# First batch's row products: all four sums kept in their own accumulators, with negated tables, instead of half sums that are joined afterwards

## The chip, the cores and the metric

The kernel runs on one core of a Trainium2 chip. The metric is the time of one execution on the device, in microseconds (us). The kernel before takes 310.63 us, the median of three runs (310.2 to 311.31). The profile is one such execution; its span, from the first to the last instruction, is 308.7 us.

## The reference, cut to what matters

Attention in chunks of 32 positions, then a Fourier mix, then a two-layer network, for 4 batches of 768 positions and 512 channels (8 heads of 64).

```python
for c in range(S // 32):                       # attention: chunk 32, 16 left, 8 right, 8 memory rows
    k_full = concat([mem_k, k[..., l_start:r_end, :]])
    v_full = concat([mem_v, v[..., l_start:r_end, :]])
    a = softmax(q_c @ k_full.T / sqrt(D))
    out[c_start:c_end] = a @ v_full
x = out.transpose(0, 2, 1, 3).reshape(B, S, 512)
mixed = real(fft(fft(x, axis=1), axis=2))      # Fourier mix over positions and channels
u = x + mixed
un = (u - mean(u)) / sqrt(var(u) + 1e-6)
y = u + max(un @ w_ch1, 0) @ w_ch2             # 512 -> 2048 -> 512
```

## The kernel before

A planner lists tasks with an engine, an estimated cost, what they come after and which buffers they take and give. It places them with a simple clock of its own and so fixes the order of each engine's program; nothing else of its clock reaches the chip. Six accumulator banks are shared by turns, value products, row and column products and the network. A pair is two heads; pairs 0 to 3 are the first batch, 4 to 7 the second, and so on. `...` marks cuts.

```python
# loads: q and k on GpSimd's DMA queue, v on SyncE's
lq = add("POOL", 0.8, lambda: e_load_q(n), [behind1, kept.get("lk"), ...], take=("qf",), moved=1.5, rank=10 * n)
lk = add("POOL", 0.8, lambda: e_load_k(n), [lq], take=("kf",), moved=1.5, rank=10 * n + 1)
lv = [add("SP", ..., lambda hh=hh: e_load_v(n, hh), ..., moved=1.6 if n < HP else 0.9) for hh in range(2)]
# GpSimd copies 32 rows of v so that neighbouring chunks overlap
ov = [add("POOL", 0.84, lambda hh=hh: e_overlap(n, hh), [lv[hh], calm], margin=mgl) for hh in range(2)]
tq = add("PE", 0.40, lambda: e_turn_q(n), [lq, ...], give=("qf",), ...)    # turns of q and k
tk = add("PE", 0.43, lambda: e_turn_k(n), [lk, ..., tq], give=("kf",), ...)
...                                                                        # scores, exp
v_ = add("PE", 0.85, lambda g=g: e_values(n, g), x_ + ov, take=("xa",), ...)   # value products
t_norm[n, g] = add("DVE", 0.78, lambda g=g: e_norm(n, g), [v_, ...])

def load_w1(after):   # four quarters on GpSimd's queue, after the last overlap copy of pair 3
    return [add("POOL", 0.7, ..., [after], moved=2.2, rank=-1) for dt in range(NDT)]
def load_w2(after):   # four quarters, into the buffer that pair 3's v held
    return [add("POOL", 0.7, lambda g=g: e_w2(g), [after], moved=2.2, rank=-1) for g in range(4)]
```

The Fourier mix is a matrix product over positions (row products, with cosine and sine tables) and one over channels (column products). Symmetry folds the channels, which gives an even (`par` 0) and an odd (`par` 1) part, and a cosine (`ab` 0) and a sine (`ab` 1) part of each. The folded values are split into a high and a low 16-bit half (`hi`, `lo`), and so are the row sums (`up` and its remainder). In the first batch the channels come in two halves `h`: pairs 0 and 3 first, pairs 1 and 2 after. The second half's sums enter the even and odd parts with equal or opposite signs.

```python
def row_products(out_, parts, ab, tab, c0, c1, first=True, last=True):
    for sp in range(2):
        for st in range(3):
            for i, part in enumerate(parts):           # hi, lo: 12 matmuls of 193 columns
                nc.tensor.matmul(out_[:, sp, :], part[:, ab, sp * 3 + st, c0:c1], tab[:, sp, st, :], ...)

def e0_edge():                                         # one row each, at channels 128 and 384
    for par, tab in ((0, cosS), (1, sinS)):
        row_products(ps_of["own", par, 1][0:1], [e128...], par, tab, 0, 1)

def e0_rows(key, ab, h):
    ps_of[key] = ps = bank([P, 2, NK], FP32, "ps0")
    row_products(ps, hl_of[0, h], ab, cosS if ab == 0 else sinS, 0, P)

def e0_keep(key, ab):                                  # first half's sums to an SBUF buffer
    nc.scalar.copy(t_of[0][:, ab, key[1]], ps_of.pop(key))
def e0_join(par, ab):                                  # plus or minus the second half's sums
    op = ALU.add if par == ab else ALU.subtract
    nc.vector.tensor_tensor(t_of[0][:, ab, par], t_of[0][:, ab, ab and par], ps_of["other", ab], op)
def e0_up(par, ab): ...                                # ScalarE: high half of the joined sums
def e0_rest(par, ab): ...                              # VectorE: remainder
```

After the column products come the residual sums with the mean (VectorE), `un` (ScalarE), four turns of `un` per tile of 128 positions (TensorE), their copies `unT`, and the network: `ph` (first products, 64 matmuls of 384 columns per half batch), relu (ScalarE), `pc` (second products, 16 of 512 columns per tile), `osb`, and the store. The network's products have the lowest rank on TensorE and fill it wherever nothing else can run. Before the network has started, dummy `warm` matmuls fill planned gaps.

Of the kernel before, what the change touches and what calls it, by code (L numbers as in the profile page):

```python
# [10 lines left out]
FP32 = mybir.dt.float32  # L11
# [24 lines left out]
class Plan:  # L36
# [13 lines left out]
    def add(self, engine, cost, emit, after=(), take=(), give=(), rank=None, moved=0.0,  # L50
            fill=False, margin=0.0):
        t = dict(engine=engine, cost=cost, emit=emit, after=[a for a in after if a is not None],
                 take=take, give=give, rank=len(self.tasks) if rank is None else rank,
                 moved=moved, fill=fill, margin=margin, last_fill=False, done=None, at=None, no=len(self.tasks),
                 bank=None)
        self.tasks.append(t)
        return t
# [77 lines left out]
def kernel(  # L135
# [15 lines left out]
    P = 128  # L151
# [41 lines left out]
    def bank(shape, dtype, name):  # L193

        return bps.tile(shape, dtype, tag="bank%d" % plan.current["bank"], name=name)
# [34 lines left out]
    cosD = wpool.tile([P, 2, HD], FP16)  # L230
    nsinD = wpool.tile([P, 2, HD], FP16)
    sinD = wpool.tile([P, 2, HD], FP16)
    c384 = cpool.tile([P, NST], FP32)
    e128 = cpool.tile([P, 2, 2, NST], FP16)
    w1_sb = wpool.tile([P, NDT, DFF], FP16)
# [271 lines left out]
# [3 lines that stand above are left out]
                for i, part in enumerate(parts):  # L510
                    nc.tensor.matmul(out_[:, sp, :], part[:, ab, sp * 3 + st, c0:c1],  # L511
                                     tab[:, sp, st, :], start=(first and sp + st + i == 0),
                                     stop=(last and sp + st + i == 4))
# [55 lines left out]
    def e0_edge():  # L569

        for par, tab in ((0, cosS), (1, sinS)):
            row_products(ps_of["own", par, 1][0:1],
                         [e128[:, i].unsqueeze(3) for i in range(2)], par, tab, 0, 1)

    def e0_ff_edge(h):

# [14 lines left out]
            nc.vector.tensor_tensor(ff[:, ab, :, 1:P], rev_ap(pq, P - 1, P - 1, [[HD, NST]]),  # L591
                                    pq[:, :, P + 1:HD], op)

    def e0_rows(key, ab, h):

        ps_of[key] = ps = bank([P, 2, NK], FP32, "ps0")
        row_products(ps, hl_of[0, h], ab, cosS if ab == 0 else sinS, 0, P)

    t_of = []

    def e0_keep(key, ab):
        if not t_of:
            t_of.append(fpool.tile([P, 2, 2, 2, NK], FP32, tag="unT", bufs=2, name="join"))
        nc.scalar.copy(t_of[0][:, ab, key[1]], ps_of.pop(key))

    def e0_join(par, ab):
        op = ALU.add if par == ab else ALU.subtract
        nc.vector.tensor_tensor(t_of[0][:, ab, par], t_of[0][:, ab, ab and par],
                                ps_of["other", ab], op)

    def e0_up(par, ab):
        up = fpool.tile([P, 2, NK, 2], FP16, tag="up", bufs=4, name="up")
        up_of[0, par, ab] = [up.rearrange("p i k s -> p i (k s)"), None, up]
        nc.scalar.copy(up[:, 0].rearrange("p k s -> p s k"), t_of[0][:, ab, par])

    def e0_rest(par, ab):
        up = up_of[0, par, ab][2]
        nc.vector.tensor_tensor(up[:, 1].rearrange("p k s -> p s k"), t_of[0][:, ab, par],
                                up[:, 0].rearrange("p k s -> p s k"), ALU.subtract)

    def e0_columns(kt, ab):

# [169 lines left out]
    def e_table_rows():  # L792

        for tab, par, s0 in ((nsinD, 0, 1.0), (sinD, 0, 1.0), (nsinD, 1, -1.0), (sinD, 1, 1.0)):
            nc.gpsimd.memset(tab[0:1, par, 0:HD:2], s0)
            nc.gpsimd.memset(tab[0:1, par, 1:HD:2], -s0)

    t_sines = []
    for i, nm in enumerate("SSD"):
        t_sines.append(add("ACT", (1.35, 1.35, 1.8)[i], lambda i=i: e_sines(i), [t_angle[nm]]))  # L800
# [4 lines left out]
    for i in range(1, NV + 1):  # L805
        t_ones[i] = add("DVE", 0.1, lambda i=i: e_ones(i),
                        [t_col, t_clear["va", i, 0], t_clear["va", i, 1]])
    t_idh = add("DVE", 0.25, lambda: nc.vector.tensor_copy(ident_h, ident), [t_id], rank=142)


# [6 lines left out]
    def attention(n):  # L817
# [6 lines left out]
        kept["lk"] = lk  # L824
        lv = [add("SP", 2.1 if hh == 0 else 1.4, lambda hh=hh: e_load_v(n, hh),
                  [t_clear.get(("va", n, 0)), t_clear.get(("va", n, 1))], rank=10 * n + 2 + hh,
                  take=("va",) if hh == 0 and n != HP - 1 else (), moved=1.6 if n < HP else 0.9) for hh in range(2)]
        first = b == 0
        calm = kept["f0"] if b == 1 else None
        mgp, mg, mgl = SPARE[b]  # L830
# [8 lines left out]
                 margin=mgp)  # L839
        kept["tk"] = tk  # L840
        mk = add("DVE", 0.2, lambda: e_mkT(n),
                 [t_mkT, kept.get("mk"), t_clear["kTb", n] if n < NKT else None,
                  kept["f0"] if n == HP + 1 else None], take=("kTb",),
                 rank=len(plan.tasks) + 400 if b == 1 else None)
        kept["mk"] = mk
        ek = add("ACT", 0.85, lambda: e_kT(n), [tk, mk], give=(("tr", tk),), margin=mg)
# [49 lines left out]

    def load_w1(after):
        return [add("POOL", 0.7, lambda dt=dt: nc.gpsimd.dma_start(
            w1_sb[:, dt, :], moe_w_ch1[ts(dt, P), :]), [after], moved=2.2, rank=-1)
            for dt in range(NDT)]  # L900

    def e_w2(g):
        if g == 0:
            w2_of.append(wpool.tile([P, NHT, DM], FP16, tag="w2", name="w2_sb"))
        nc.gpsimd.dma_start(w2_of[0][:, ts(g, 4), :], w2v[:, ts(g, 4), :])  # L905

    def load_w2(after):
        return [add("POOL", 0.7, lambda g=g: e_w2(g), [after], moved=2.2, rank=-1)
                for g in range(4)]


# [28 lines left out]
    def part_of_first(add, t_rest):  # L940
        nrm = [[t_norm[i, g] for g in range(2)] for i in range(HP)]
        ff = hi = None
        rows, keep, t_join = {}, {}, {}
        for h in range(2):
            pq = [None]
            for i in range(2):
                pq.append(add("DVE", 1.15, lambda h=h, i=i: e0_pq(h, i),
                              nrm[2 * h + i] + [pq[-1]], take=("fold",) if i == 0 else ()))
            prev = pq[-1]
            if h == 1:  # L950
                ed = add("POOL", 0.8, e0_edge_parts, [pq[1]], rank=-3)
                ed = add("PE", 1.94, e0_edge, [ed, rows["own", 0, 1], rows["own", 1, 1]])
                for par in range(2):
                    own = rows["own", par, 1]
                    keep[par, 1] = add("ACT", 0.6, lambda par=par: e0_keep(("own", par, 1), 1),
                                       [ed], give=(("acc", own),))
            fe = add("DVE" if h else "POOL", 0.25 if h else 0.4, lambda h=h: e0_ff_edge(h),
                     [pq[-1]], take=("fold",), rank=None if h else -4)
            for ab in range(2):
                ff = add("DVE", 0.95, lambda h=h, ab=ab: e0_ff(h, ab), [fe, prev],  # L960
                         give=("fold",) if ab == 1 else ())
                prev = ff
                ht = ("hT", "hl")[h]
                hi = add("ACT", 0.85, lambda h=h, ab=ab: e_hi(0, h, ab), [ff, hi],
                         take=(ht,) if ab == 0 else ())
                lo = add("DVE", 0.96, lambda h=h, ab=ab: e_lo(0, h, ab), [hi],
                         give=("fold",) if ab == 1 else ())
                more = [kept["tk0"]] + t_sines if h == 0 else []
                for par in range(2 if (h, ab) == (0, 1) else 1):
                    key = ("own", par, ab) if h == 0 else ("other", ab)  # L970
                    end = (h, ab) == (1, 1) or (h, ab, par) == (0, 1, 1)
                    rows[key] = add("PE", 1.1, lambda h=h, ab=ab, key=key: e0_rows(key, ab, h),
                                    [lo] + more, take=("acc",), give=(ht,) if end else ())
            if h == 0:
                keep[0, 0] = add("ACT", 0.6, lambda: e0_keep(("own", 0, 0), 0), [rows["own", 0, 0]],
                                 take=("unT",), give=(("acc", rows["own", 0, 0]),))
                t_norm[2, 1]["after"].append(ff)
        join = up = None
        for ab in range(2):
            other = rows["other", ab]  # L980
            for par in (1 - ab, ab):
                t_join[par, ab] = join = add(
                    "DVE", 0.6, lambda par=par, ab=ab: e0_join(par, ab),
                    [keep[ab and par, ab], other, join],
                    give=(("acc", other),) if par == ab else ())
        for ab in range(2):
            for par in (1 - ab, ab):
                up = add("ACT", 0.5, lambda par=par, ab=ab: e0_up(par, ab), [t_join[par, ab], up],
                         take=("up",))
                t_rest[par, ab] = add("DVE", 0.45, lambda par=par, ab=ab: e0_rest(par, ab), [up],  # L990
                                      give=("unT",) if par and ab else ())
        kept["f0"] = lo

    def fourier(b):
# [149 lines left out]
```

## Time and profile before

| what | value |
|---|---|
| time, median of 3 runs | 310.63 us |
| span of the profiled run | 308.7 us |
| TensorE busy | 290.8 us (94%) |
| VectorE, ScalarE, GpSimd busy | 176.8, 167.8, 69.7 us |
| warm matmuls | 182, 14.4 us |
| ps matmuls (row products) | 264 |
| DMA moved | 24.49 MB, mean 79 GB/s |

The busy time of TensorE is a sum of instructions; the slices show where it is spent. The mean of 79 GB/s hides that nearly all loads come in the first quarter of the span. The chain of waits that ended last gives 76% of the span to TensorE and 8% to DMA, nearly all of that to `w_sb`, the weights' loads; and the chain is listed in order of time, so one can see where that share lies. An idle time in a row is the time of that engine just before the row's instructions, with what ended it; the releaser is inferred.

### The profile page before, as it was taken

Reading aid. Unit: us, or ns where it says so; the run is one execution under the profiler, and the core shown is the slowest. Engines: PE = TensorE matmul, PEld = TensorE weight load, DVE = VectorE, ACT = ScalarE, POOL = GpSimd, SP = SyncE. Lnnn points to the kernel's source line nnn. Section 1 sums busy time; section 2 is a strip of 40 time slices with the busy share of each in tenths; the row PEclk is TensorE's granted clock in tenths of the full one; section 3 lists DMA queues with packets and bytes.
Section 4 is the critical chain, followed back from the end, with each engine's and each line's share of the span. In section 5 each row is a group of like instructions: output and inputs, shape, how many; then the busy total and the mean of one; then the engine's idle time right before and its main releaser. Section 6 shows DMA issues by size and latency. Waiting matters only on the chain.

```text
span 308.7 us, 7849 instructions
## 1 busy us (share of the span) xinstructions
PE 290.8 (94%) x3327; PEld 193.9 (63%) x3327; DVE 176.8 (57%) x364; ACT 167.8 (54%) x300; POOL 69.7 (23%) x121
## 2 busy tenths in 40 slices
PE   8697999199999999999999999999999999999995
PEld 8586887076565756866668755767564554554644
DVE  7949978433149993689988989837800101002002
ACT  9966585437756388484585634652371360540720
POOL 7567721454352730032400020000100000000000
PEclk9999999669999999999999999999999999999999
DMA  6999999987679420033300001000100101101001
GB/s 84 166 159 202 195 200 196 199 151 119 94 149 192 98 55 2 2 95 83 101 2 2 2 34 71 0 2 34 46 24 34 71 0 55 49 0 68 36 34 68
DMA packets 42313, 24.49 MB, mean 79 GB/s; under 512 B 30375, under 2 KB 38823, under 8 KB 42279
## 3 DMA queue, kind: packets, MB, share of 16 engines
q0 software_dynamic: 9344, 10.49, 21.5%
q1 hardware_dynamic: 29479, 7.34, 13.0%
q10 hardware_dynamic: 3456, 6.16, 5.3%
q8 instruction: 26, 0.43, 0.6%
q14 instruction: 8, 0.07, 0.1%
HBM read 28.11 MB, written 6.29 MB: 111 GB/s over the span
## 4 chain that ended last, share of the span: by engine, by line
PE 76%; DMA 8%; DVE 7%; ACT 3%; issue 2%; POOL 2%; POOLq 0%
PE ph L685 27%; PE pc L699 24%; PE xa L437 7%; DMA w_sb<-in_moe_w_ch_dram 7%; PE pm L546 5%; PE ps L511 5%; PE sc L382 2%; PE tp L664 1%; ACT e L425 1%; PE trq L346 1%; PE trk L361 1%; DMA qf<-in_q_dram 1%; PE pc_half L707 1%; DVE lo L504 1%; POOL w_sb L905 1%
## 5 line engine op out<-in xcount | busy, mean ns | idle before, releaser
L692 ACT ACTIVATE hT<-ph 128x384 f16<-128x384 f32 x128 | 62.1, 491 | 66.0 <-PE ph L685 64.1
L685 PE MATMUL ph<-unT,w_sb 128*128 128x384 f16 x512 | 89.4, 328 | 0.7 <-ACT hT L692 0.6
L699 PE MATMUL pc<-w_sb,hT 128*128 128x512 f16 x368 | 84.8, 379 | 0.6 <-DVE unT L670 0.6
L685 PEld LDWEIGHTS <-w_sb 128*128 128x128 f16 x512 | 48.4, 98 | 33.4 <-issue 2.0
L699 PEld LDWEIGHTS <-hT 128*128 128x128 f16 x368 | 34.5, 98 | 38.3 <-issue 0.6
L727 DVE SCALAR_TENSOR_TENSOR osb<-pc,rstd,xsb 128x512 f32<-128x512 f32 x23 | 17.2, 748 | 71.7 <-PE pc L699 71.6
L339 POOL COPY va<-va 32x780 f32<-32x780 f32 x30 | 29.6, 1007 | 35.6 <-DMA va<-in_v_dram 35.1
L437 PE MATMUL xa<-va,e 128*64 128x65 f32 x720 | 28.0, 231 | 7.5 <-POOL va L339 6.6
L437 PEld LDWEIGHTS xa<-va,e 128*64 128x64 f32 x720 | 24.4, 143 | 12.7 <-POOL va L339 7.4
L390 ACT ACTIVATE e<-sc,mbias 128x384 f32<-128x384 f32 x48 | 25.2, 577 | 10.3 <-PE sc L382 9.8
L658 ACT ACTIVATE un<-xsb,mu_s 128x512 f16<-128x512 f32 x18 | 12.8, 720 | 15.7 <-DVE mu_s L652 15.6
L447 DVE RECIPROCAL zs<-xa 128x6 f32<-128x6 f32 x32 | 6.1, 189 | 21.7 <-PE xa L437 21.6
L448 DVE TENSOR_TENSOR xsb<-xa,zs 128x384 f32<-128x384 f32 x32 | 17.8, 558 | 1.1
L676 POOL TENSOR_SCALAR rstd<-mu_s 128x6 f32<-128x6 f32 x4 | 1.0, 245 | 70.7 <-DVE osb L727 42.0
L651 DVE BATCH_NORM_STATS2 st<-xsb 128x6 f32<-128x512 f32 x24 | 16.6, 690 | 0.6
L499 ACT CAST hi<-ff 128x768 f16<-128x768 f32 x14 | 11.4, 830 | 9.3 <-DVE ff L488 7.8
L310 POOL DMA_DIRECT2D qf<-in_q_dram x16 | 10.6, 660 | 23.7 <-PE trq L346 14.5
L504 DVE TENSOR_TENSOR lo<-ff,hi 128x768 f16<-128x768 f32 x14 | 14.4, 1042 | 2.4 <-ACT hi L499 2.4
L460 PE MATMUL warm<-zeros 128*128 128x128 bf16 x182 | 14.4, 242 | 1.0 <-DVE zero L247 1.0
L645 DVE TENSOR_TENSOR xsb<-pm,xsb 128x512 f32<-128x512 f32 x18 | 12.1, 672 | 5.2 <-PE pm L546 5.2
L351 ACT COPY qT<-trq 128x768 bf16<-128x768 bf16 x14 | 11.1, 795 | 6.4 <-PE sc L382 5.7
L371 ACT COPY kTb<-trk 128x832 bf16<-128x832 bf16 x16 | 13.4, 854 | 0.4 <-DVE osb L727 0.4
(147 smaller groups left out, 398.5 us busy)
## 6 DMA issues: line engine op xcount, KB each, us to landing
out_dram<-osb ACTq DMA_DIRECT2D x23, 256.0 KB
va<-in_v_dram SPq DMA_DIRECT2D x30, 176.0 KB
w_sb<-in_moe_w_ch_dram POOLq DMA_DIRECT2D x8, 512.0 KB, 13.2
qf<-in_q_dram POOLq DMA_DIRECT2D x16, 192.0 KB, 4.3
kf_all<-in_k_dram POOLq DMA_DIRECT2D x16, 192.0 KB, 5.8
va<-in_mem_v_dram SPq DMA_DIRECT2D x30, 24.0 KB
va<-in_v_dram SPq DMA_DIRECT2D x15, 28.0 KB
last<-in_v_dram SPq DMA_DIRECT2D x2, 176.0 KB
```

Source lines behind the costliest of these rows:

```text
L339: nc.gpsimd.tensor_copy(v1[0:32, 1:NB, 0:D + 1], v1[96:128, 0:NT, 0:D + 1])
L390: nc.scalar.activation(e1[:, :, :, ts(half, 32)], sc[:, :, 0:6, ts(half, 32)], AFT.Exp, bias=mbias[:, half:half + 1], scale=1.0 / math.sqr ...
L437: nc.tensor.matmul(xa[64 * half:64 * half + 64, st, hh, 0:65], e1[:, hh, t6, :], v1[:, 6 * g + t6 + 1, 0:65], start=True, stop=True)
L448: nc.vector.tensor_tensor(xs[b][:, 3 * g:3 * g + 3, 2 * pr * D:(2 * pr + 2) * D] .rearrange("p s (h d) -> p s h d", h=2), xa[:, :, :, 0:D] ...
L504: nc.vector.tensor_tensor(lo[:, ab].rearrange(fl), ff_of[b, par][:, ab].rearrange(fl), hi[:, ab].rearrange(fl), ALU.subtract)
L511: nc.tensor.matmul(out_[:, sp, :], part[:, ab, sp * 3 + st, c0:c1], tab[:, sp, st, :], start=(first and sp + st + i == 0), stop=(last and ...
L546: nc.tensor.matmul(pm[:, par, :], lhs, rhs[:, par, :], start=(im == 0), stop=(im == 3))
L651: nc.vector.bn_stats(st6, xs[b][:, kt, :])
L685: nc.tensor.matmul(ph[:, 0:384], w1_sb[:, dt, ts(ht, P)], unT_of[b][:, dt, sh * 384:(sh + 1) * 384], start=(dt == 0), stop=(dt == NDT - 1))
L692: nc.scalar.activation(hT_of[b, sh][:, ht, :], ph_of.pop((b, sh, ht))[:, 0:384], AFT.Relu, bias=0.0, scale=-1.0)
L699: nc.tensor.matmul(pc_of[b, sh, stl], hT_of[b, sh][:, ht, ts(stl, P)], w2_of[0][:, ht, :], start=(ht == 0), stop=(ht == NHT - 1))
L727: nc.vector.scalar_tensor_tensor(osb, pc_of.pop((b, sh, stl)), rstd_of[b][:, st:st + 1], xs[b][:, st, :], ALU.mult, ALU.add)
```

## The change

Each half of the first batch now makes all four row products (`par`, `ab`) of its own, and the second half adds to the first half's accumulators. Where the second half must enter with the opposite sign, its products take a negated table, made once at the start. So the copies to SBUF and the joins go, and the split reads the accumulators directly, as in the later batches. The two edge rows are added between the halves into the same accumulators. The planner's figures for the weights' and v's transfer times are other ones, and the memory keys' copy of pair 5 no longer waits for the first batch's last split.

```diff
     def e0_edge():
         for par, tab in ((0, cosS), (1, sinS)):
-            row_products(ps_of["own", par, 1][0:1],
-                         [e128[:, i].unsqueeze(3) for i in range(2)], par, tab, 0, 1)
+            row_products(ps_of[0, par, 1][0:1],
+                         [e128[:, i].unsqueeze(3) for i in range(2)], par, tab, 0, 1,
+                         False, False)
...
-    def e0_rows(key, ab, h):
-        ps_of[key] = ps = bank([P, 2, NK], FP32, "ps0")
-        row_products(ps, hl_of[0, h], ab, cosS if ab == 0 else sinS, 0, P)
-    def e0_keep(key, ab): ...
-    def e0_join(par, ab): ...
-    def e0_up(par, ab): ...
-    def e0_rest(par, ab): ...
+    def e0_rows(par, ab, h):
+        if h == 0:
+            ps_of[0, par, ab] = bank([P, 2, NK], FP32, "ps0")
+        ps = ps_of[0, par, ab]
+        turned = h == 1 and par != ab
+        tab = neg_of[0][:, ab] if turned else (cosS if ab == 0 else sinS)
+        row_products(ps, hl_of[0, h], ab, tab, 0, P, h == 0, h == 1)
...
+    def e_neg(i):
+        if i == 0:
+            neg_of.append(fpool.tile([P, 2, 2, 3, NK], FP16, tag="unT", bufs=2, name="neg"))
+        nc.vector.tensor_scalar(neg_of[0][:, i]..., (cosS, sinS)[i]..., -1.0, None, ALU.mult)
...
+    t_neg = [add("DVE", 0.4, lambda i=i: e_neg(i), t_sines[:2], rank=140 + i,
+                 take=("unT",) if i == 0 else ()) for i in range(2)]
...
         lv = ...
-                  ..., moved=1.6 if n < HP else 0.9) for hh in range(2)]
+                  ..., moved=1.6) for hh in range(2)]
...
         mk = add("DVE", 0.2, lambda: e_mkT(n),
-                 [t_mkT, kept.get("mk"), t_clear["kTb", n] if n < NKT else None,
-                  kept["f0"] if n == HP + 1 else None], take=("kTb",),
+                 [t_mkT, kept.get("mk"), t_clear["kTb", n] if n < NKT else None], take=("kTb",),
...
-            w1_sb[:, dt, :], moe_w_ch1[ts(dt, P), :]), [after], moved=2.2, rank=-1)
+            w1_sb[:, dt, :], moe_w_ch1[ts(dt, P), :]), [after], moved=3.2, rank=-1)
...
-        return [add("POOL", 0.7, lambda g=g: e_w2(g), [after], moved=2.2, rank=-1)
+        return [add("POOL", 0.7, lambda g=g: e_w2(g), [after], moved=3.5, rank=-1)
...
-                for par in range(2 if (h, ab) == (0, 1) else 1):
-                    key = ("own", par, ab) if h == 0 else ("other", ab)
-                    rows[key] = add("PE", 1.1, ..., [lo] + more, take=("acc",), ...)
-            if h == 0:
-                keep[0, 0] = add("ACT", 0.6, ...)
-                t_norm[2, 1]["after"].append(ff)
-        ...                          # joins, then splits, then remainders
+                for par in range(2):
+                    rows[par, ab] = rw = add(
+                        "PE", 1.0, lambda h=h, par=par, ab=ab: e0_rows(par, ab, h),
+                        [lo] + ([kept["v0" if (par, ab) == (1, 1) else "tk0"]] + t_sines if h == 0 else
+                                [rows[par, ab], t_neg[ab], ed]),
+                        take=("acc",) if h == 0 else (), ...)
+                    if h == 0:
+                        held[par, ab] = rw
+                    else:
+                        up = add("ACT", 0.6, lambda ...: e_up(0, par, ab), [rw], take=("up",))
+                        t_rest[par, ab] = add("DVE", 0.6, lambda ...: e_rest(0, par, ab), [up],
+                                              give=(("acc", held[par, ab]),))
```

More of the change, by code (lines that the diff above doesn't have):

```diff
@@ L232 @@
     sinD = wpool.tile([P, 2, HD], FP16)
+    neg_of = []
     c384 = cpool.tile([P, NST], FP32)
@@ L592, in e0_ff @@
                                     pq[:, :, P + 1:HD], op)
-    def e0_rows(key, ab, h):
-        ps_of[key] = ps = bank([P, 2, NK], FP32, "ps0")
-        row_products(ps, hl_of[0, h], ab, cosS if ab == 0 else sinS, 0, P)
[L599 to L619, printed above, removed]
+    def e0_rows(par, ab, h):
[5 more added lines that the diff above has]
+        row_products(ps, hl_of[0, h], ab, tab, 0, P, h == 0, h == 1)
     def e0_columns(kt, ab):
@@ L796, in e_table_rows @@
             nc.gpsimd.memset(tab[0:1, par, 1:HD:2], -s0)
+    def e_neg(i):
+        if i == 0:
+            neg_of.append(fpool.tile([P, 2, 2, 3, NK], FP16, tag="unT", bufs=2, name="neg"))
+        fl = "p a b c -> p (a b c)"
+        nc.vector.tensor_scalar(neg_of[0][:, i].rearrange(fl), (cosS, sinS)[i].rearrange(fl),
+                                -1.0, None, ALU.mult)
     t_sines = []
@@ L826, in attention @@
                   [t_clear.get(("va", n, 0)), t_clear.get(("va", n, 1))], rank=10 * n + 2 + hh,
-                  take=("va",) if hh == 0 and n != HP - 1 else (), moved=1.6 if n < HP else 0.9) for hh in range(2)]
+                  take=("va",) if hh == 0 and n != HP - 1 else (), moved=1.6) for hh in range(2)]
         first = b == 0
@@ L942, in part_of_first @@
         ff = hi = None
-        rows, keep, t_join = {}, {}, {}
+        rows = {}
+        held = {}
         for h in range(2):
@@ L951, in part_of_first @@
                 ed = add("POOL", 0.8, e0_edge_parts, [pq[1]], rank=-3)
[L952 to L956, printed above, removed]
+                ed = add("PE", 1.94, e0_edge, [ed, rows[0, 1], rows[1, 1]])
             fe = add("DVE" if h else "POOL", 0.25 if h else 0.4, lambda h=h: e0_ff_edge(h),
@@ L967, in part_of_first @@
                          give=("fold",) if ab == 1 else ())
-                more = [kept["tk0"]] + t_sines if h == 0 else []
-                for par in range(2 if (h, ab) == (0, 1) else 1):
-                    key = ("own", par, ab) if h == 0 else ("other", ab)
-                    end = (h, ab) == (1, 1) or (h, ab, par) == (0, 1, 1)
-                    rows[key] = add("PE", 1.1, lambda h=h, ab=ab, key=key: e0_rows(key, ab, h),
-                                    [lo] + more, take=("acc",), give=(ht,) if end else ())
@@ L974, in part_of_first @@
-            if h == 0:
-                keep[0, 0] = add("ACT", 0.6, lambda: e0_keep(("own", 0, 0), 0), [rows["own", 0, 0]],
-                                 take=("unT",), give=(("acc", rows["own", 0, 0]),))
-                t_norm[2, 1]["after"].append(ff)
[L978 to L991, printed above, removed]
+                for par in range(2):
+                    rows[par, ab] = rw = add(
+                        "PE", 1.0,
+                        lambda h=h, par=par, ab=ab: e0_rows(par, ab, h),
+                        [lo] + ([kept["v0" if (par, ab) == (1, 1) else "tk0"]] + t_sines if h == 0 else
+                                [rows[par, ab], t_neg[ab], ed]),
+                        take=("acc",) if h == 0 else (),
+                        give=((ht,) if par == 1 and ab == 1 else ()) +
+                        (("unT",) if (h, par, ab) == (1, 1, 1) else ()))
+                    if h == 0:
+                        held[par, ab] = rw
+                    else:
+                        up = add("ACT", 0.6, lambda par=par, ab=ab: e_up(0, par, ab), [rw],
+                                 take=("up",))
+                        t_rest[par, ab] = add("DVE", 0.6, lambda par=par, ab=ab:
+                                              e_rest(0, par, ab), [up], give=(("acc", held[par, ab]),))
```

## The prediction

> **What bounds the kernel now.** I read the page's forty slices first, then windows cut at the places where the slices change, then the chain of waits, then the timelines of TensorE and GpSimd around the one hole. From the page:
>
> ```profile
> PE   8697999199999999999999999999999999999995
> PEclk9999999669999999999999999999999999999999
> DMA  6999999987679420033300001000100101101001
> ```
>
> TensorE is full from slice 9 to the end. Before that it has one hole, slice 7 (about 54 to 62 us), and the granted clock drops there and in the slice after. The DMA engines are full from slice 1 to slice 7. Windows with the columns stretch, length, busy times of PE, PEld, DVE, ACT, POOL, granted clock, DMA share, GB/s:
>
> ```profile
> 54.36:60.68 6.32, 0.00 (x0) 0.00 (x1) 3.12 (x10) 2.95 (x6) 2.14 (x4) 0.69 1.22 198
> 60.68:66.70 6.02, 5.72 (x72) 4.54 (x72) 2.96 (x8) 1.16 (x3) 3.91 (x5) 0.50 1.06 181
> 66.70:305.40 238.70, 236.97 (x2392) 147.64 (x2388) 125.27 (x234) 123.36 (x230) 33.52 (x38) 1.00 0.22 53
> ```
>
> So 6.32 us of nothing, then 6.02 us at exactly half clock, then 238.7 us with only 1.73 us idle. From 66.7 us on the time is TensorE work and nothing else. What ended the hole is in the timelines of TensorE and of GpSimd (start, us, then the idle time before and its releaser):
>
> ```profile
> 60.68 0.48 PE L437 MATMUL xa<-va,e 128*64 128x65 f32 x4 [6.32 <-POOL va L339]
> ...
> 49.11 0.63 POOL L310 DMA_DIRECT2D qf<-in_q_dram  x1 [3.88 <-PE sc L382]
> 52.24 0.63 POOL L315 DMA_DIRECT2D kf_all<-in_k_dram  x1 [2.50 <-DMA w_sb<-in_moe_w_ch_dram]
> 55.61 0.63 POOL L310 DMA_DIRECT2D qf<-in_q_dram  x1 [2.75 <-DMA w_sb<-in_moe_w_ch_dram]
> 59.12 0.63 POOL L315 DMA_DIRECT2D kf_all<-in_k_dram  x1 [2.88 <-DMA va<-in_v_dram]
> 59.80 4.94 POOL L339 COPY va<-va 32x780 f32<-32x780 f32 x6
> ```
>
> TensorE waits for the value product of pair 4 (the first of the second batch), that waits for GpSimd's overlap copies of its v, and those stand in GpSimd's program behind four DMA issues for q and k of pairs 8 and 9. [...] each waits for the one eight before it, here a quarter of w2: the landings, each the issue time plus its time to landing, are 48.6, 51.6, 55.1 and 58.5 us, and the issues follow 0.5 to 0.6 us later. I take the releasers "PE sc" and "DMA va" here for mislabelled; the landings fit all four. The v data itself is early: pair 4's loads are issued by 28.4 us. The hole is thus an **order on GpSimd**, not missing data.
>
> [...] 0.50 after 6.32 us idle; it took 6.02 us to come back, and the idle gaps of at most 0.9 us in the first 34 us left the clock at 1.00. [...] the chain of waits has 36 row products in 3.12 us, 86.7 ns each, and I use that. [...] q of pair 6, issued at 37.95 us behind w2, landed 21.4 us later at 59.35, after w2's last quarter. [...]
>
> **The change part by part.**
>
> *Removed.* Three ScalarE copies into the join buffer (481 ns each, 1.4 us) and four VectorE joins (555 ns each, 2.1 us). Both engines have slack everywhere but in the stage at 34 to 54 us, where they head the chain: join, split, remainder. It also drops 30 warm matmuls net (about 60 ns each, 1.8 us), which filled idle time only.
>
> *Added.* Each half now makes all four row products of its own instead of three and two: 8 groups of 12 matmuls against 5, so 36 more at 86.7 ns = **3.1 us of TensorE**. Two VectorE negations of the tables, 1158 elements each; by the reversal copy (768 elements of the same type, 393 ns) at most about 0.6 us each, 1.2 us in all, at about 15 us, where VectorE has 1.8 us idle before its next turn copy. I count 0.3 us for them, which goes into waiting for DMA.
>
> *Moved.* The planner also gets other costs (w1 3.2 and w2 3.5 us per quarter in place of 2.2; the landings of the quarters are about 2.8 and 3.3 us apart), and the built order differs after 41 us. In GpSimd's program the overlap copies of pairs 4 and 5 now stand **ahead of** the issues for pair 9. In TensorE's program the turns of pair 5 move from 40.6 us to just ahead of the value product of pair 4; all 64 first products and one more turn of u stand behind it.
>
> *The new time of that value product.* GpSimd: the issue at 52.24 us is as before (same queue, same landings), ends at 52.9, two copies of 0.83 us follow: 54.6. TensorE from 34.1 us: 24 row products 2.08, turns of pair 4 0.83, 12 more 1.04, six warm 0.35, 12 more 1.04, 24 edge products 2.08, 48 of the second half 4.16: 45.7. The last split and remainder (605 and 593 ns) and handovers: 47.1, against 46.35 for the last remainder before. From there the third turn of u took 5 us before (51.2 to 51.6), so about 52.1; the scores 0.28 and the turns of pair 5 0.83 make 53.2. So TensorE waits about 1.5 us, for GpSimd, and **resumes at about 54.7 us** rather than 60.68. A gap of 1.5 us should leave the clock alone.
>
> *The half clock.* What ran from 60.68 to 66.7 at half rate, at the rates later in the same trace: 48 value products 1.70 us against 3.14 (its 0.29 us wait apart), first products 0.65 against 1.40, two turns of u 0.55 against 0.85, turns of q 0.40 against 0.78. Lost: 2.9 us.
>
> *The sum.* From the resumption to the end before: 308.7 - 60.68 = 248.0 us, less 2.9 (clock), less the second wait of 0.29: 244.9. More remains behind that point now: 8 first products at 0.1625 us (64 take 10.40) and one turn of u, 0.28: 1.6. So 54.7 + 244.9 + 1.6 = 301.2 us of span. The 3.1 us of new row products lie before 47 us, in the stage that waits for w2 anyway, and cost nothing at the end. The times are 1.9 us over the span (310.63 against 308.7): 303.1. The later order is new everywhere, and such an order before kept 1.7 us of small waits; I add 0.7 us: **303.8 us**.
>
> **Rivals.** *The hole only moves.* The DMA queue is full to about 67 us either way, q and k of pairs 6 to 9 land from 59.35 to 67.0 us, and TensorE now comes to them sooner. For it: an in-order engine stops at any late load. Against it: in the built order 64 first products (10.4 us), value products and scores lie between 54.7 us and the turns of pair 6, so these come at about 68 us. If wrong, up to 6 us come back, and with them perhaps the half clock: 306 to 310.
>
> *TensorE is the bound and got more work.* 36 products more, 3.1 us on an engine busy 94%: about 313 or 314. For it: everything after 66.7 us is TensorE work. Against it: these products stand before the hole and take the place of warm ones and of idling.
>
> *The clock drops all the same*, because the gap is longer than I think or the stretch before it is thin: the clock share in the window from 50 to 55 us would show it. 2.9 us back: about 306.7.
>
> *The chain before the hole gets longer.* Four accumulators are held from 36 to 46 us, which leaves two banks for turns and values. If the columns come 3 us later than I have them, the resumption comes later one for one, since GpSimd is then no longer the last: about 305.
>
> **Range and chances.** The hole's cause is plain and its removal can be read in the built order, so I put most weight on a gain; the size hangs on the resumption time (plus or minus 2 us), the clock (2.9 us) and new waits in the later order (minus 1 to plus 5). All of it well gives 301, half of it lost gives 308. The 2% line lies at 304.4, just above my value: 0.58 for faster by over 2%, 0.37 within 2%, 0.05 slower.
>
> **What the profile after would show.** Right: no PE idle of over 3 us between 50 and 62 us; the first overlap copy for pair 4 at about 53 us, right behind the k issue at about 52.2; clock 0.95 or more from 50 to 67 us; TensorE in row products to about 45.7 us; 264 + 36 matmuls in the row groups; the idle total after 67 us still under 3 us. Wrong: a wait of TensorE at turns of q or k (the loads bound it), a wait at column products (the split and remainder bound it), or a resumption near 60 us although the copies were done. The prediction fails if waits of several us appear in the second to fourth batch, whose order I took as no better or worse than before.

## The result and the profile after

The changed kernel takes 305.43 us (median of four runs, 304.99 to 306.07) against 310.41 us before: ratio 0.9838, 95% interval 0.9806 to 0.987. The profiled run has a span of 303.9 us. All medians and ratios here are of fast runs; one run of `a_early` below, at 307.82 us, is a slow one. The slices of its page:

```profile
PE   8797999799999999999899999999999999999995
PEclk9999999999999999999999999999999999999999
DMA  6999999995996513213200001001000101101001
```

The hole in slice 7 is gone, and so is the dip of the clock. The loads fill the DMA engines just as before up to that point; nothing was gained there. (They are less confined to the first quarter than I said ahead: in the page of the kernel before, slices 11 and 12, about 85 to 100 us, still have 149 and 192 GB/s.) The timelines of TensorE and of GpSimd at the place of the hole (start, us, and at the end the idle time before with its releaser):

```profile
54.10 0.34 PE L439 MATMUL xa<-va,e 128*64 128x65 f32 x4 [1.38 <-POOL va L341]
54.88 0.80 PE L439 MATMUL xa<-va,e 128*64 128x65 f32 x20 [0.45 <-POOL va L341]
...
52.54 0.63 POOL L317 DMA_DIRECT2D kf_all<-in_k_dram  x1 [2.76 <-PE trq L348]
53.22 3.18 POOL L341 COPY va<-va 32x780 f32<-32x780 f32 x4
56.35 0.63 POOL L312 DMA_DIRECT2D qf<-in_q_dram  x1
59.15 0.63 POOL L317 DMA_DIRECT2D kf_all<-in_k_dram  x1 [2.16 <-PE tp L648]
```

Before, GpSimd issued at 52.24, 55.61 and 59.12 us and copied at 59.80. Now it issues at 52.54, copies at 53.22, and waits for an earlier landing again only at 59.15. TensorE starts the value product at 54.10 us and is free of waits at 54.88, where it used to be free at 61.46 (0.78 us after the first value product at 60.68). The windows from the resumption to the end of TensorE's work (length, busy times of PE, PEld, DVE, ACT, POOL, granted clock, DMA share, GB/s):

```profile
54.88:61.00 6.12, 5.57 (x73) 3.78 (x74) 5.65 (x18) 4.46 (x9) 3.58 (x5) 1.00 1.23 198
61.00:300.60 239.60, 237.33 (x2405) 147.04 (x2402) 126.95 (x233) 124.39 (x233) 36.16 (x39) 1.00 0.26 58
```

Full clock in both, where the 6 us after the hole ran at 0.50 before. So much is comparison. Which part of the change did it, the row products or the order of two instructions, only further runs can tell.

### The profile page after: what moved, and what is told of

It reads as the page before. It is cut to its first block, busy times and chain, and to the rows that moved or that the text cites. A ratio compares the mean times of both kernels' runs of the same rounds, so it can differ in the third digit from the quotient of the medians.

```text
span 303.9 us, 7854 instructions
## 1 busy us (share of the span) xinstructions
PE 290.2 (95%) x3333; PEld 193.2 (64%) x3333; DVE 177.5 (58%) x362; ACT 166.3 (55%) x297; POOL 72.9 (24%) x121
## 4 chain that ended last, share of the span: by engine, by line
PE 76%; DMA 10%; DVE 6%; ACT 3%; POOL 2%; issue 1%; ACTq 0%; POOLq 0%; SPq 0%
PE pc L683 25%; PE ph L669 24%; PE xa L439 6%; PE pm L548 5%; DMA w_sb<-in_moe_w_ch_dram 5%; PE ps L513 4%; DMA va<-in_v_dram 3%; DMA kf_all<-in_k_dram 2%; PE sc L384 2%; PE tp L648 2%; PE trq L348 2%; PE trk L363 2%; ACT e L427 2%; PE warm L462 1%; PE pc_half L691 1%
## 5 line engine op out<-in xcount | busy, mean ns | idle before, releaser
L683 PE MATMUL pc<-w_sb,hT 128*128 128x512 f16 x368 | 85.7, 380 | 0.0
L341 POOL COPY va<-va 32x780 f32<-32x780 f32 x30 | 31.4, 1063 | 31.2 <-DMA va<-in_v_dram 30.8
L439 PE MATMUL xa<-va,e 128*64 128x65 f32 x720 | 26.6, 225 | 2.7 <-POOL va L341 2.2
L439 PEld LDWEIGHTS xa<-va,e 128*64 128x64 f32 x720 | 23.2, 137 | 8.3 <-issue 4.0
L528 ACT CAST up<-ps 128x386 f16<-128x386 f32 x16 | 9.7, 606 | 17.7 <-PE ps L513 17.6
L317 POOL DMA_DIRECT2D kf_all<-in_k_dram x16 | 10.1, 634 | 15.2 <-PE trk L363 5.2
L462 PE MATMUL warm<-zeros 128*128 128x128 bf16 x152 | 12.3, 246 | 1.0 <-DVE zero L249 1.0
```

The costliest lines, as they stand in the source:

```text
L341: nc.gpsimd.tensor_copy(v1[0:32, 1:NB, 0:D + 1], v1[96:128, 0:NT, 0:D + 1])
L439: nc.tensor.matmul(xa[64 * half:64 * half + 64, st, hh, 0:65], e1[:, hh, t6, :], v1[:, 6 * g + t6 + 1, 0:65], start=True, stop=True)
L462: nc.tensor.matmul(warm_of[0], zeros, zeros, start=True, stop=True)
L683: nc.tensor.matmul(pc_of[b, sh, stl], hT_of[b, sh][:, ht, ts(stl, P)], w2_of[0][:, ht, :], start=(ht == 0), stop=(ht == NHT - 1))
```

## The experiments

The theory: the hole was made by the order of GpSimd's program, and the row products matter only because they moved a turn of TensorE and with it, in the planner's clock, two DMA issues. (That last step is read from the planner's lists, where the buffers for q and k of pair 9 come free with the turns of pair 5; no run moves that turn alone.) The rivals: the shorter chain (no copies, no joins), and the planner's figures. To move single instructions, the list that the planner returns was rearranged before the programs were written, so that all else kept its place.

**The swap in the kernel before** (`b_order`).

```diff
+        late = [lq of pair 9, lk of pair 9]
+        # taken out of the list and put back right behind the overlap copies of pair 5
```

> The kernel before, with one swap in GpSimd's program and nothing else: the two issues for q and k of pair 9 stand behind the overlap copies of pairs 4 and 5, as in the changed kernel. Theory (the order on GpSimd made the hole): the first overlap copy for pair 4 starts at about 53.2 us instead of 59.8, the value products of pair 4 run at about 54.9 us at full clock, a new wait of about 1.6 us appears at the turn of q of pair 6 (its q lands at 59.35 us); span about 301.4 us, time about 303.3 (302 to 305). Rival (the shorter chain without copies and joins made the gain): no change, 310.4.

It took 305.57 us, ratio 0.9853 (0.979 to 0.9916). TensorE and GpSimd in its timelines:

```profile
55.31 0.34 PE L437 MATMUL xa<-va,e 128*64 128x65 f32 x4 [0.83 <-POOL va L339]
56.10 1.50 PE L437 MATMUL xa<-va,e 128*64 128x65 f32 x44 [0.44 <-POOL va L339]
61.01 0.53 PE L346 MATMUL trq<-ident_b,qf 96*64 96x96 bf16 x16 [2.21 <-DMA qf<-in_q_dram]
...
53.76 0.63 POOL L315 DMA_DIRECT2D kf_all<-in_k_dram  x1 [2.52 <-PE ph L685]
54.43 3.18 POOL L339 COPY va<-va 32x780 f32<-32x780 f32 x4
```

The old row products, joins and all, with two issues moved: the same time as the whole change. The new wait at q of pair 6 came where it was expected, 2.2 us rather than 1.6. The four landings of w2 are 1.5 us later in this run than in that of before (the issue for k of pair 8, which waits for one of them, at 53.76, not 52.24), which is most of the 2.2 us by which its span of 303.6 us exceeds the expected one.

**The swap undone in the changed kernel** (`a_order`).

```diff
+        block = [lq, lk of pair 9] + [overlap copies of pairs 4 and 5]
+        # taken out of the list and put back, in this order, ahead of the value product of pair 4
```

> The changed kernel, with the same swap undone: the issues for q and k of pair 9 ahead of the overlap copies of pairs 4 and 5; all else as in the changed kernel. Theory (order on GpSimd): first overlap copy at about 59.8 us, hole of about 7 us before the first value product of the second batch, half clock for about 6 us after it; 6.2 us of wait and 2.9 us of clock more than the changed kernel: time about 314.5 (313 to 316), slower than the kernel before because 1.9 us more of work stand behind the hole. Rival (shorter chain): still about 305.4.

314.12 us, ratio 1.0119 (1.0081 to 1.0157): slower than the kernel before, with all four row products in place. Its windows across the place:

```profile
52.70:59.82 7.12, 0.08 (x5) 0.01 (x1) 4.76 (x17) 1.03 (x2) 2.14 (x4) 0.72 1.22 198
59.82:66.00 6.18, 5.74 (x49) 3.62 (x51) 1.54 (x4) 2.18 (x5) 3.90 (x5) 0.50 1.03 167
```

The hole of 7 us and the 6 us at half clock are both back. Together the two runs leave the shorter chain no gain of its own to explain: the order gives about 5 us without the new row products, and undoing it costs 8 to 9 us with them.

**The planner's figures alone, and all but the figures** (`b_fig`, `a_fig`).

```diff
 # b_fig: the kernel before
-    ..., [after], moved=2.2, rank=-1)        # w1, w2
+    ..., [after], moved=3.2, rank=-1)        # w1; w2: 3.5; v: 1.6 for all pairs
-    [..., kept["f0"] if n == HP + 1 else None], take=("kTb",)
+    [...], take=("kTb",)
 # a_fig: the changed kernel with the same lines the other way round
```

> The kernel before with only the planner's figures and the one dependence of the change (w1 3.2, w2 3.5, v 1.6, no wait of the memory keys' copy of pair 5), its row products unchanged. Theory (order on GpSimd): in the built order the issues of pair 9 still stand ahead of the copies of pair 4, so the hole stays; 310 plus or minus 1.5. Rival (the planner's figures made the gain): about 305.5.

> The changed kernel's row products with the planner's figures and the dependence of the kernel before. Theory (order on GpSimd): in the built order the copies of pairs 4 and 5 stand ahead of the issues of pair 9, so no hole: 305.5 plus or minus 1.5. Rival (the planner's figures made the gain): about 310.

`a_fig` took 306.81 us, ratio 0.9896 (0.9861 to 0.9931), as the theory has it: GpSimd copies at 52.93 us, and TensorE waits 2.02 us for the first value product. The 1.4 us between it and the changed kernel are not settled, as the intervals overlap. `b_fig` keeps the hole (6.27 us), but at 316.92 us, ratio 1.0216 (1.0157 to 1.0274), it is 7 us slower than the theory said and 11 us slower than the rival. The first two lines are from the timelines of `a_fig`, the others from the timeline, the slices and the timeline of `b_fig`:

```profile
53.82 0.34 PE L439 MATMUL xa<-va,e 128*64 128x65 f32 x4 [2.02 <-POOL va L341]
52.93 3.17 POOL L341 COPY va<-va 32x780 f32<-32x780 f32 x4
...
61.28 0.48 PE L437 MATMUL xa<-va,e 128*64 128x65 f32 x4 [6.27 <-POOL va L339]
PEclk9799999789999999999899999999999999999999
151.94 0.38 PE L664 MATMUL tp<-ident_h,un 128*128 128x128 f16 x4 [0.58 <-ACT hT L692]
153.61 0.81 PE L685 MATMUL ph<-unT,w_sb 128*128 128x384 f16 x4 [1.29 <-DVE unT L670]
155.00 3.67 PE L685 MATMUL ph<-unT,w_sb 128*128 128x384 f16 x12 [0.58 <-ACT hT L692]
```

The figures change the order of the later batches. From 140 to 170 us TensorE is busy for 24.76 us of 30, against 29.77 in the kernel before, as first products now stand right behind the copies and the relu that they wait for, and the clock drops once more, for 3.4 us. So an order of the planner can cost 5 us in the later batches; the change had no such stretch.

**The clock by itself** (`b_warm`).

```diff
 def e_values(n, g):
     xa_of[n, g] = xa
+    if (n, g) == (HP, 0):
+        for i in range(100):       # on zeros, into the bank that the value product then overwrites
+            nc.tensor.matmul(xa...[:, 0:P], zeros, zeros, start=True, stop=True)
```

> The kernel before, with 100 dummy matmuls on zeros put right ahead of the first value product of the second batch, so that TensorE is busy for about 5.6 us of its 6.3 us hole; nothing else. Theory (half of the loss was the clock): the hole is filled, the copies still end it at about 60.7 us, but the granted clock stays at 1.00 after it; 2.9 us less: time about 307.7 (306.8 to 308.6). Rival (the clock did not cost what I worked out, because the work after the hole waits for copies and loads anyway): 310 to 311.

309.22 us, ratio 0.9961 (0.9939 to 0.9983): 1.2 us gained with an interval of 0.5 to 1.9 us, under half of the 2.9 expected. TensorE's timeline, and the windows around the end of the hole:

```profile
55.04 5.75 PE L434 MATMUL xa<-zeros 128*128 128x128 bf16 x100
62.18 1.50 PE L441 MATMUL xa<-va,e 128*64 128x65 f32 x44 [0.44 <-POOL va L339]
...
54.00:60.00 6.00, 6.00 (x100) 5.67 (x98) 4.25 (x14) 4.03 (x8) 0.78 (x2) 1.00 1.23 199
60.00:66.00 6.00, 4.94 (x106) 3.94 (x103) 2.83 (x8) 1.46 (x3) 5.56 (x8) 1.00 1.21 199
```

The clock stays at 1.00 here, but not in all twenty runs of this kernel: ten have a mean granted clock of 0.999 or 1.00 and a median of 308.33 us, the other ten lie at 0.982 to 0.994 with a median of 310.41. So the 1.2 us are a mixture; where the clock stayed up, the gain is about 2 us (308.33 against 310.53 for the kernel before beside it). The profiles agree. In this one the copies come 0.7 us later than in that of before; from the second of the two waits to the end of the span it takes 245.2 us (307.4 - 62.18) against 247.2 (308.7 - 61.46), so 2.0 us less. The order is the same, so the two can be laid side by side: from that wait to the scores at 65.28 us (67.07 before) `b_warm` needs 3.10 us instead of 5.61, and 0.5 us of these 2.5 are lost again at 150.81 us, where a row product waits 0.75 us for VectorE instead of 0.23. So the half clock cost 2.5 us where it ran and 2.0 us at the end, not 2.9.

**Twice the added work** (`a_extra`, and `a_extra2` beside the changed kernel itself).

```diff
+        if h == 0 and (par, ab) != (0, 0):
+            row_products(ps, hl_of[0, h], ab, tab, 0, P)      # made once for nothing
         row_products(ps, hl_of[0, h], ab, tab, 0, P, h == 0, h == 1)
```

> The changed kernel with 36 more row products in the first half of the first batch: three of the four groups of 12 are made twice, the first time for nothing. This doubles the TensorE work that the change added (3.1 us). Theory (that work lies ahead of a wait for GpSimd): TensorE is ready for the first value product of the second batch at about 55.8 us instead of 52.7, where it now starts at 54.1 and is free of waits at 54.9; 1.0 us more: time about 306.4 (305.8 to 307.2). Rival (TensorE is the bound everywhere): 3.1 us more, 308.5.

> The changed kernel with 36 row products made twice, once more beside the changed kernel. Theory (2.0 us of the 3.1 us go into the wait for the copies): 1.1 us more than the changed kernel, 306.5. Rival (TensorE is the bound everywhere): 3.1 us more, 308.5.

The first took 307.63 us (ratio 0.9913, 0.9879 to 0.9946), which lies between the two theories. Beside the second stood the changed kernel (`after2`).

> The changed kernel as it is, timed beside the next three so that differences of 1 us can be read: 305.4 (304.8 to 306.2).

`after2` took 306.07 us (ratio 0.9867, 0.9826 to 0.9908), `a_extra2` 307.37 (0.9893, 0.9852 to 0.9935): 1.3 us more where the theory said 1.1 and the rival 3.1, though the intervals of these two overlap. The timeline of `a_extra2` shows how:

```profile
54.78 0.54 PE L363 MATMUL trk<-ident_b,kf_all 104*64 104x104 bf16 x16
55.15 0.88 PE L439 MATMUL xa<-va,e 128*64 128x65 f32 x24
```

The turns of pair 5 now end after the two copies for pair 4, and the value product follows without a wait. So 36 products fit into the time that TensorE would have waited, nearly all: the first product of the network after them starts at 55.96 us, against 55.48 in `after2`.

**The copies one issue earlier still** (`a_early`, and `a_early2` beside the changed kernel).

```diff
+        block = [overlap copies of pairs 4 and 5]
+        # put ahead of the issue for k of pair 8
```

> The changed kernel, with the overlap copies of pairs 4 and 5 one more issue earlier on GpSimd: ahead of the issue for k of pair 8, all else the same. Theory (the order on GpSimd): the copies start at about 49.8 us, TensorE goes from the turns of pair 5 straight to the value product at 52.7 us without the waits of 1.4 and 0.45 us: time about 303.6 (302.8 to 304.8), if v of pair 4 has landed by 50 us. Rival (v lands later than that, or the other chains are no faster): about 305.4.

> The changed kernel with the copies of pairs 4 and 5 ahead of the issue for k of pair 8, once more beside the changed kernel. Theory (order on GpSimd): the two waits of 1.4 and 0.45 us go: 1.8 us less than the changed kernel, 303.6. Rival (other chains take their place): the same as the changed kernel.

304.13 us (ratio 0.9787, 0.9737 to 0.9837; the median of five runs) and 305.25 us (0.9827, 0.9788 to 0.9866). Beside `after2`, `a_early2` is 0.8 us less, and the intervals overlap, so the size is not settled. From the page and the timelines of `a_early2`:

```profile
PEclk9799999999999999999999999999999999999999
...
10.28 0.56 PE L363 MATMUL trk<-ident_b,kf_all 104*64 104x104 bf16 x16 [2.73 <-DMA kf_all<-in_k_dram]
...
54.43 0.88 PE L439 MATMUL xa<-va,e 128*64 128x65 f32 x24
...
49.85 3.17 POOL L341 COPY va<-va 32x780 f32<-32x780 f32 x4
```

The waits before the value product are gone as expected, since v of pair 4 had landed by 49.85 us. But TensorE came there 2.2 us later than in `after2` (the turn of k of pair 5 starts at 54.06 us, against 51.84): the clock dropped in slice 1, after the first load's wait (0.59 from 11 to 15 us). All five runs of `a_early2` have the mean clock of 0.994 that such a drop leaves (3.4 us at half clock in 304), but only three of the six of `after2`, and those took 306.45, 306.89 and 307.63 us. Like beside like the gain is thus nearer to the 1.8 us expected, on few runs.

**The order mended in the kernel before** (`b_best`).

```diff
+        early = [overlap copies of pairs 4 and 5]       # ahead of the issue for k of pair 8
+        late  = [lq, lk of pair 9]                      # right behind that issue
+        turns = [turns of pair 6 with their copies, lq, lk of pair 10]
+        # put behind the value products of pair 5
```

> The kernel before (its joins and its fewer row products kept) with GpSimd's order mended: copies of pairs 4 and 5 ahead of the issue for k of pair 8, issues of pair 9 behind them, and on TensorE the turns of pair 6 behind the value products of pair 5, so that they do not wait for their loads. Theory (only the order matters): TensorE goes on at 54.4 us without a hole; 54.4 + 241.5 of work and small waits + 3.4 of end = 299.3 us of span, 301.2 of time (300.2 to 303): faster than the changed kernel by about 4 us, as its order behind the hole has fewer changes between kinds of products and less work. Rival (the row products in own accumulators are worth something in themselves): no faster than the changed kernel with the same mending, 303.6.

301.8 us, ratio 0.9731 (0.9685 to 0.9777), the fastest of all kernels here, and faster than `a_early2`, the changed kernel with its copies moved likewise (the intervals lie apart; that of `a_early` overlaps), against the rival. How much of that distance is the clock at 10 us, which dropped in `a_early2` and not in the profile of `b_best`, and how much fewer cuts and less work, no run separates. TensorE's timeline and the two windows that showed the hole before:

```profile
54.55 1.62 PE L437 MATMUL xa<-va,e 128*64 128x65 f32 x48
63.05 0.51 PE L346 MATMUL trq<-ident_b,qf 96*64 96x96 bf16 x16
...
54.36:60.68 6.32, 6.04 (x112) 4.59 (x110) 6.01 (x20) 6.07 (x13) 1.94 (x5) 1.00 1.22 196
60.68:66.70 6.02, 5.50 (x107) 3.76 (x105) 2.71 (x7) 3.86 (x8) 1.66 (x3) 1.00 1.22 196
```

No hole, no half clock, and no wait at the turn of q of pair 6. It computes with the joins and the 264 row products that the change removed and replaced.

## Why the prediction was right

It said 303.8 us, with 301 if all went well and 308 if half was lost; it was 305.43. The ratio's interval, a reduction of 1.3 to 1.9%, lies within the 2% line, which I had given 0.37; I gave 0.58 to the side beyond it.

*The cause of the hole*: right, and shown both ways by `b_order` and `a_order`. *The resumption*: TensorE was to be in row products until 45.7 us and ready at 53.2; in the trace they end at 45.3, the turns of pair 5 at 52.7, and the value product starts at 54.1 with a second wait that ends at 54.9. I had 54.7 and no second wait, though before has one of 0.29 us; start and second wait together make 54.55, so this term was right. *The added products cost nothing at the end*: supported by the 1.38 us that TensorE still waited in the changed kernel, and by `a_extra2`, in which as many again cost 1.3 us in the medians and 0.5 us in the profiles, the part that no longer fits into the wait. The two negations took 0.45 and 1.10 us instead of at most 0.6 each; they lie before that wait too.

*The half clock*: that a gap of 1.5 us would leave the clock alone was my estimate. It held: the clock reads 1.00 after the wait of 1.38 us in the changed kernel, and 0.50 after the one of 6.32 us before. (I misread two places: the trace of before has a gap of 1.70 us at 9.4 us, not 0.9 at most in the first 34 us, and it left the clock at 1.00; and the clock was at 0.50 not only for the 6.02 us behind the hole but for 10.24 us, from 56.78 us, within the hole, to 67.02 us.) The size of the loss, 2.9 us, was too large: in `b_warm` the stretch was 2.5 us shorter and the end came 2.0 us sooner. I had set the slow stretch against rates taken from long rows of one kind, and part of what I counted as lost was not the clock's, since short rows need it at 1.00 too: the 48 value products, which I had at 1.70 us, took 1.84 (0.34 + 1.50) in `b_warm`, the turns of q 0.53 and not 0.40. By groups, the same 576 value products were busy for 22.54 us from the hole's end to the last product before and for 21.12 after, the 160 turns of q for 5.57 and 5.23, the first products, less the 8 added ones, for 87.97 and 87.6: 2.1 us in all.

*The rest of the path*: this term was too small. From 54.55 us (the start of the value product plus the second wait) to the end of the span I had 244.9 + 1.6 = 246.5 us; the trace has 303.9 - 54.55 = 249.35. Of these 2.85 us, 0.3 are one group of scores that had run before the hole and now runs after it, which I overlooked. Small waits of TensorE from there to its last product grew from 1.7 to 2.8 us (by the windows), 1.1. The over-sized clock term makes up 0.8 (2.9 against 2.1). And the new order cuts the second products into 37 groups instead of 32; most cuts cost, as two rows of the chain of waits of the changed kernel show (start, length):

```profile
69.98 0.97 PE pc L683 x4
...
290.17 6.91 PE pc L683 x32
```

Four alone take 0.97 us in most of their groups (0.86 in some), four in a row of 32 take 0.86. The busy time of the second products is 85.67 us against 84.79, another 0.9; five cuts at 0.11 us would make 0.55 of that, and the rest is not traced to single cuts. That is 3.1 us for 2.85, which is as near as these sums come. My allowance for all this was 0.7 us.

*The rivals*: the chain before the hole did not get longer (45.3 us for 45.7). The hole did not move, since the turns of pair 6 came at 69.5 us, long after their loads. In `b_order`, where only 5 us of work stood between, the wait did appear (2.21 us at the turn of q of pair 6): the rival was sound, and the built order decided it.

## What to carry to other kernels

When one engine's program both issues DMA and computes, look at what stands behind an issue that waits for the queue: here copies of 0.8 us, their data there or nearly so, waited 7 us behind issues whose loads were wanted more than 20 us later (the turn of q of pair 9 ran at 82.6 us before). A rewrite that changes a planner's order should be tested against the order alone, since the order, not the arithmetic, carried the whole gain here (`b_order`), and mending it further in the old kernel was worth more (`b_best`, 301.8 us). And count the cuts between kinds of products when a filler stream is interleaved.

## What was not expected of the hardware

I had not expected the clock to drop at about 10 us, where TensorE waits for the first k in every kernel. In the eight profiled runs in which the clock stayed at 1.00 from 11 to 15 us, this wait was 1.60 to 2.43 us. In the four in which it was 2.51, 2.64, 2.73 and 2.79 us, the clock there was 0.57 to 0.61. One more run (`a_extra`) had 0.71 with a wait of 1.83 us; there the clock was down already at the first product after the wait (0.84 from 7.6 to 11 us).

So the length of a single wait does not sort these runs: 2.43 us left the clock at 1.00 (`a_order`), 1.83 us did not (`a_extra`). The traces hold the times at which the granted clock changed. In the trace of before it fell 2.42 us into the hole and was at 0.50 for 10.24 us, three times 3.41 us. Four cases in windows of 3.41 us: two rows of before, the second over those 10.24 us, then pairs from `a_order`, `a_extra` and `b_fig` (columns as above):

```profile
53.37:56.78 3.41, 0.99 (x9) 0.56 (x7) 3.24 (x13) 3.28 (x8) 0.63 (x1) 1.00 1.22 197
56.78:67.02 10.24, 6.04 (x76) 4.79 (x76) 3.76 (x11) 2.01 (x5) 5.42 (x7) 0.50 1.11 186
8.03:11.44 3.41, 1.63 (x37) 1.56 (x38) 3.18 (x8) 3.30 (x7) 0.73 (x6) 1.00 1.01 175
11.44:14.86 3.42, 3.42 (x78) 2.94 (x75) 3.03 (x9) 3.39 (x6) 3.35 (x6) 1.00 0.83 119
6.50:9.91 3.41, 1.62 (x34) 1.28 (x32) 3.31 (x6) 3.30 (x6) 0.35 (x3) 1.00 1.08 173
9.91:13.32 3.41, 3.37 (x40) 3.24 (x41) 2.47 (x10) 3.41 (x6) 2.59 (x9) 0.50 0.72 109
151.38:154.79 3.41, 1.19 (x8) 0.65 (x8) 3.41 (x7) 0.82 (x2) 1.93 (x2) 1.00 0.56 128
154.79:158.21 3.42, 3.21 (x11) 1.53 (x11) 3.38 (x7) 1.82 (x5) 1.71 (x2) 0.50 0.00 0
```

In the first window of each pair TensorE was idle for 2.42 us (before), 1.78 us (`a_order`), 1.79 us (`a_extra`) and 2.22 us (`b_fig`). In the second the clock read 0.50 in before, `a_extra` and `b_fig` and 1.00 in `a_order`. The windows of before, `a_extra` and `b_fig` meet where the clock changed; those of `a_order` meet 13 times 3.41 us ahead of the change in its hole, at 55.8 us. Of the wait of 2.43 us in `a_order`, 0.65 us lie ahead of its first window; the 1.83 us of `a_extra` lie nearly all in one; in `b_fig` several waits, none over 1.29 us, add up. These are four cases in one kernel, two of them 0.01 us apart, and no run was made to test whether the sum decides. In `after2` the three runs with a mean clock of 0.994 took 306.45 to 307.63 us and the three with 0.998 to 1.00 took 305.47 to 305.69, which is one reason why differences of 1 us needed runs side by side.
